# Attention and two feed-forward layers on one core: a fifth group in seven-product form, and weight blocks converted during the scores

## The chip, the cores and the metric

The kernel runs on one core of one Trainium2 chip. The metric is device time in microseconds of one execution; the kernel before has a median of 1001.72 us over three runs (1000.77 to 1002.63). The engines named below are TensorE (PE; PEld is its weight load), VectorE (DVE), ScalarE (ACT), GpSimd (POOL) and SyncE (SP, which issues nearly all transfers).

## The reference

Three stages over 6016 tokens of 256 channels, all in float32. The weights come in as float64, seen as pairs of 32-bit words.

```
qn = q / (norm(q over tokens) + 1e-6);  kn = likewise
s  = kn^T @ qn / tau                    # 256 x 256
a  = exp(s - max);  a = a / (a.sum + 1e-9)
x  = v @ a                              # 6016 x 256
x  = (relu(x @ w_in1) ** 2) @ w_out1    # d_ff 2048
y  = leaky(x @ w_in2, 0.01) @ w_out2
```

## The kernel before

**The scores.** q and k are loaded in 12 tiles (`qk`), eleven of 4 x 128 tokens (1 MB) and one of 3 x 128. TensorE accumulates k and q into the two halves of the scores (`sT`, L386), two records for one f32 product. ScalarE squares each tile (`sq`, L371), VectorE adds it to a running sum (`acc`, L376). At the last tile VectorE folds `acc` (L378) into `sums` (L379, L380), and TensorE sums it over the partitions (`pn`, four products with `ones`, eight records, L360); in TensorE's program these stand before the last two thirds of the last tile's score products. Then come the square root, reciprocals, the scaled scores, their transposes, the exponentials `e`, their transposes `eT`.

**Weights.** A float64 block is turned into float32 by a `Unit` (L124 on): ScalarE scales the high words (L143, `cm`), VectorE shifts, joins the sign, joins the low words (L146, L149, L153: the triple), ScalarE rounds to the high part (L192), VectorE takes the rest as the low part (`low`, L110). Each value is so held as two parts, and a product is three matmuls (high-high, high-low, low-high). `later` holds steps that are put behind the next tile's squares or additions. There are 16 blocks for the first layer: for each of 8 groups of 256 hidden channels an input block (`i`) and an output block (`o`).

**The fold.** x = v @ a is never formed: a is multiplied into w_in1, group by group (`pw`, L252, 12 matmuls of 256 columns), and scaled by the softmax's sums.

**The pairs.** The tokens go in six pairs of 448 or 512 tokens times two; each layer runs over the six pairs, each pair over the 8 groups. A group's first product, 256 channels by 256 hidden by two halves, is either plain, 8 block products of 3 matmuls (24, `h`, L704), or in seven-product form (Strassen's, 21 matmuls in the banks `ha` and `hb`, L543). The latter needs sums of weight blocks (VectorE L207 to L210 and a rounding of `wi`), sums of token blocks (`xr`), copies on ScalarE (L1504) and three additions on VectorE (L550). In the first pair the groups below `N0` are plain.

**What sets the order.** Up to the fold of group 0 the order is that of the code. Behind it a planner (`build`, `simulate`) places every instruction of the two layers on its engine by costs and due times, several rounds of it, and the best round is written out. `convert` gives a weight block's steps to it. SP issues transfers in program order, with eight lanes; a transfer waits for the one before it on its lane, and a tile of q and k for one of five buffers (`AHEAD`), free when TensorE and ScalarE are done with the tile. Three buffers (`wst`) hold raw weight blocks.

Of the kernel before, what the change touches and what calls it, by code (L numbers as in the profile page):

```python
# [28 lines left out]
def attn_moe_moe2(  # L29
# [12 lines left out]
    nc = tc.nc  # L42
# [192 lines left out]


    tiles = [(t0, min(G, T - t0)) for t0 in range(0, T, G)]
    PIECES = {0: ((0, 1), (1, 1), (2, 1), (3, 1)), **{n: ((0, 2), (2, 2)) for n in (1, 2, 3)}}
    NS = len(tiles)
    AHEAD = 5  # L240
    sT = [bank("ab"[j], f"sT{j}") for j in range(KC)]
# [52 lines left out]
    def converted(units):  # L294

        for u in units:
            later[ACT].append(u.scaled)
            yield
            for step in (u.shifted, u.sign, u.high):
                step()  # L300
                if step == u.high:
                    later[ACT].append(u.round)
                    later[ACT].append(lambda u=u: later[DVE].append(u.low))
                yield

    def run(steps, n):
        for _ in range(n):
            next(steps, None)
# [4 lines left out]
    with (  # L313
# [17 lines left out]
        def load_qk(n):  # L331
            t = qk[n] = att4.tile([P, 2, G, C], F32, tag="qk", name="qk")
            for i, m in pieces(n):

                t0 = (tiles[n][0] + i) * P
                for a, x in enumerate((q, k)):
                    src = x[0][t0 : t0 + m * P, :].rearrange("(p g) c -> p g c", g=m)
                    (nc.scalar if a and n == 0 else nc.sync).dma_start(t[:, a, i : i + m], src)  # L338

        for n in range(AHEAD):  # L340
            load_qk(n)
            if n == 3:
                first_i[0].load()
        tiny = small[:, 6, 0:1]
        nc.vector.memset(tiny, 1e-36)
        nc.scalar.activation(small[:, 7, 0:1], ones, AF.Square)
# [2 lines left out]

        for _ in range(6):  # L350
            nc.tensor.matmul(warm[:, :P], zeros, zeros, start=True, stop=True)
        steps = [converted([u]) for u in first_i]

        STEPS = {2: 1, 3: 3}

        def norm_sums():

# [7 lines left out]
        for n, (t0, g) in enumerate(tiles):  # L365
            t = qk.pop(n)
            last_tile = n == NS - 1

            sq = att2.tile([P, 2, G, C], F32, tag="sq", name="sq") if n else acc
            for i, m in pieces(n):  # L370
                nc.scalar.activation(part(sq, i, m), part(t, i, m), AF.Square)  # L371
            if last_tile:
                nc.scalar.activation(small[:, 7, 0:1], ones, AF.Sqrt)
            flush(ACT)
            if n:
                tt(part(acc, 0, g), part(acc, 0, g), part(sq, 0, g), op=ALU.add)  # L376
            if last_tile:
                tt(part(acc, 0, 2), part(acc, 0, 2), part(acc, 2, 2), op=ALU.add)  # L378
                tt(sums_[:, :C], acc[:, 0, 0], acc[:, 0, 1], op=ALU.add)  # L379
                tt(ordered(sums_[:, C:]), in_order(acc[:, 1, 0]), in_order(acc[:, 1, 1]), op=ALU.add)  # L380
            flush(DVE)
            for i in range(g):
                if last_tile and i == g - 2:
                    norm_sums()
                for j in range(KC):
                    nc.tensor.matmul(  # L386
                        sT[j][:, :C],
                        t[:, 0, i, j * P : (j + 1) * P],
                        t[:, 1, i],
                        start=n == 0 and i == 0,  # L390
                        stop=last_tile and i == g - 1,
                    )
            run(steps[0], STEPS.get(n, 0))
            if n + AHEAD < NS:
                load_qk(n + AHEAD)
            elif n + AHEAD == NS:
                first_i[1].load()
                load_first_v(0)
                load_first_v(1)
                nc.sync.dma_start(tau_sb, tau.partition_broadcast(P))  # L400
                first_o.load()
                others[0].load()

        xa, xb = x_tile(2, 1, 0), x_tile(1, 1, 0)

# [24 lines left out]

        nc.vector.reciprocal(rtau, tau_sb)

        run(steps[1], 1)
        flush(ACT)
        run(steps[1], 2)
        y, m, z, r = (small[:, i] for i in range(4))
        nc.scalar.activation(y, pn[:, :4], AF.Sqrt, bias=tiny, scale=0.25)
        nc.scalar.activation(small[:, 7, 0:1], ones, AF.Exp)
# [10 lines left out]
        sTs = [att.tile([P, C], F32, name=f"sTs{j}") for j in range(KC)]  # L449
        ts(ordered(sTs[0]), in_order(sT[0][:, :C]), r[:, 0:1], rtau, op0=ALU.mult, op1=ALU.mult)  # L450
        nc.scalar.activation(ordered(sTs[1]), in_order(sT[1][:, :C]), AF.Copy, scale=rq1)
        run(steps[1], 1)
        others[1].load()
        s = [bank("e", "s0"), bank("y3", "s1")]
        x_transpose(0, 0, "y1")
        x_transpose(1, 0, "y2", range(2))
# [421 lines left out]
    TAIL = 12  # L878
    TURNS = 14
    FIRST_MIXED = min([p for L, p in GROUPS if L == 1], default=0)  # L880
    CONV_BEGIN, CONV_END = 1.4, 4
    N0 = 4
    FOLD_AFTER = "F1"
    LOAD = 22
    VDUE = 30, 60
# [101 lines left out]
    def build(base):  # L987
# [12 lines left out]
        def T(*a, **k):  # L1000
            return Task(*a, **k)
# [55 lines left out]
            return t  # L1057

        whl_done = {0: None, 1: None}
        for i, u in enumerate([first_o, *others]):  # L1060
            n = u.g - 1 if u.kind == "i" else u.g + 1
            m, at0 = in_pair0(n)
            due = at0(m["fold"] if u.kind == "i" else m["second"][u.g > 0][0])
            t = convert(u, due - 35 - (0 if i else 10), loaded=wst_b.get(i))
            if u.kind == "i":
                whl_done[u.g] = t
            else:
                wo_ready[1, 0, u.g] = t
# [875 lines left out]
```

## Time and profile before

| | |
|---|---|
| median of three runs | 1001.72 us |
| the profiled execution: time, span | 1002.93 us, 1001.1 us |
| TensorE busy | 994.6 us, 99% of the span |
| VectorE busy | 901.4 us, 90% |
| ScalarE busy | 804.4 us, 80% |
| granted TensorE clock, mean | 1.000 |
| share of TensorE in the chain that ended last | 97% |

A matmul's row shows its latency (0.38 us for 512 columns), while a new one begins every 0.23 us, so records overlap and a merged row of n is shorter than n times the mean. Idle time stands in brackets ahead of a row, with what ended it.

### The profile page before, as it was taken

The numbers are of one execution on the slowest core, as the hardware profiler recorded it, in microseconds if no ns is written. First come the engines' busy times: TensorE is split into PE (matmuls) and PEld (weight loads), VectorE is DVE, ScalarE is ACT, GpSimd is POOL, SyncE is SP. The second block draws the span as 40 slices with busy tenths as digits, with TensorE's granted clock in tenths as the row PEclk, the third lists the DMA queues.
The fourth block names the chain that finished last, engine by engine and source line by source line (L and its number), as shares of the span: only waits on it lengthen the run. The fifth ranks groups of instructions, "written<-read, shape, count | busy, mean of one in ns | idle before, by whom it ended". The sixth has DMA issues, their size and how long they took to land.

```text
span 1001.1 us, 13148 instructions
## 1 busy us (share of the span) xinstructions
PE 994.6 (99%) x4528; PEld 837.3 (84%) x4528; DVE 901.4 (90%) x1314; ACT 804.4 (80%) x1184; POOL 0.7 (0%) x6
## 2 busy tenths in 40 slices
PE   9999999999999999999999999999999999999998
PEld 7888888887888888998888888888888888998887
DVE  4899999988988977999999999999999999998985
ACT  6799978877878777888898888779788788887773
POOL 0000000000000000000000000000000000000000
PEclk9999999999999999999999999999999999999999
DMA  9786559788978967965665665666577586676553
GB/s 339 281 253 205 200 193 287 266 308 296 332 284 294 318 249 265 316 219 206 223 209 200 229 215 202 201 217 226 172 219 233 182 239 227 210 233 220 195 143 84
DMA packets 160946, 234.97 MB, mean 235 GB/s; under 512 B 53232, under 2 KB 97264, under 8 KB 158576
## 3 DMA queue, kind: packets, MB, share of 16 engines
q1 hardware_dynamic: 160160, 233.48, 69.0%
q8 instruction: 36, 0.59, 0.2%
q10 hardware_dynamic: 720, 0.66, 0.2%
q14 instruction: 30, 0.25, 0.1%
HBM read 187.70 MB, written 46.40 MB: 234 GB/s over the span
## 4 chain that ended last, share of the span: by engine, by line
PE 97%; DMA 2%; DVE 0%; ACT 0%; ACTq 0%; issue 0%; SPq 0%
PE y L543 37%; PE ha L543 21%; PE hb L543 16%; PE yA L543 7%; PE yF L543 3%; PE hc L543 3%; PE sT L386 3%; PE he L543 2%; PE h L704 2%; PE pw L252 1%; DMA qk<-in_k_dram 1%; DMA qk<-in_q_dram 1%; PE y L587 0%; DVE o L552 0%; ACT e L472 0%; ACTq L338 0%
## 5 line engine op out<-in xcount | busy, mean ns | idle before, releaser
L543 PE MATMUL y<-g,wo 128*128 128x512 f32 (+1 forms) x1344 | 350.5, 387 | 0.0
L543 PEld LDWEIGHTS y<-g,wo 128*128 128x128 f32 x1344 | 252.1, 188 | 49.5 <-DVE wo L110 0.4
L543 PE MATMUL ha<-x,wi 128*128 128x512 f32 (+1 forms) x960 | 265.6, 385 | 0.0
L110 DVE TENSOR_TENSOR g<-c,g 128x1024 fp32r<-128x1024 f32 (+1 forms) x192 | 228.0, 1197 | 18.7 <-ACT g L674 13.9
L543 PEld LDWEIGHTS ha<-x,wi 128*128 128x128 f32 x960 | 180.0, 188 | 33.8 <-ACT c L1504 0.7
L543 PE MATMUL hb<-x,wi 128*128 128x512 f32 (+1 forms) x720 | 199.6, 386 | 0.1
L543 PEld LDWEIGHTS hb<-x,wi 128*128 128x128 f32 x720 | 134.3, 188 | 26.2 <-DVE c L550 1.7
L1612 DVE TENSOR_TENSOR c<-c 128x512 f32<-128x512 f32 (+1 forms) x208 | 139.9, 672 | 7.1 <-ACT c L691 1.2
L1587 ACT CAST g<-c 128x1024 fp32r<-128x1024 f32 (+1 forms) x104 | 105.2, 1023 | 5.1 <-PE y L543 2.4
L110 DVE TENSOR_TENSOR b<-c,b 128x512 fp32r<-128x512 f32 (+1 forms) x156 | 102.5, 668 | 2.0 <-ACT b L1605 1.7
L1605 ACT CAST b<-c 128x512 fp32r<-128x512 f32 (+1 forms) x156 | 93.1, 608 | 10.5 <-DVE c L1612 4.7
L681 ACT ACTIVATE c<-c 128x1024 f32<-128x1024 f32 (+1 forms) x96 | 100.0, 1043 | 1.5
L674 ACT CAST g<-c 128x1024 fp32r<-128x1024 f32 (+1 forms) x88 | 91.7, 1044 | 1.6
L1504 ACT COPY w<-ha 128x512 f32<-128x512 f32 (+1 forms) x80 | 46.2, 577 | 49.9 <-PE ha L543 49.6
L691 ACT ACTIVATE c<-c 128x512 f32<-128x512 f32 (+1 forms) x98 | 60.7, 621 | 8.8 <-DVE c L552 8.5
L1504 ACT COPY u<-ha 128x512 f32<-128x512 f32 (+1 forms) x80 | 46.0, 575 | 9.8 <-PE ha L543 6.9
L110 DVE TENSOR_TENSOR x<-xr,x 128x1024 fp32r<-128x1024 f32 (+3 forms) x47 | 49.1, 1051 | 0.6 <-ACT x L1261 0.6
L386 PE MATMUL sT<-qk 128*128 128x256 f32 x188 | 42.1, 382 | 1.4 <-DMA qk<-in_k_dram 1.3
L543 PE MATMUL yA<-g,wo 128*128 128x512 f32 (+1 forms) x156 | 42.9, 383 | 0.0
L543 PE MATMUL yF<-g,ws 128*128 128x512 f32 (+1 forms) x156 | 42.9, 383 | 0.0
L543 PE MATMUL y<-b,ws 128*128 128x512 f32 (+1 forms) x156 | 42.9, 383 | 0.0
L543 PE MATMUL y<-b,wo 128*128 128x512 f32 (+1 forms) x156 | 42.8, 383 | 0.0
(137 smaller groups left out, 1202.4 us busy)
## 6 DMA issues: line engine op xcount, KB each, us to landing
wi<-wi SPq DMA_DIRECT2D x88, 896.0 KB, 5.6
wo<-wo SPq DMA_DIRECT2D x84, 512.0 KB, 4.5
ws<-wo SPq DMA_DIRECT2D x120, 128.0 KB, 4.0
wst<-in_moe_w_in_dram SPq DMA_DIRECT2D x16, 512.0 KB, 6.0
wst<-in_moe_w_out_dram SPq DMA_DIRECT2D x16, 512.0 KB, 6.8
wi<-wis SPq DMA_DIRECT2D x8, 896.0 KB, 6.1
wo<-wis SPq DMA_DIRECT2D x7, 1024.0 KB, 7.6
wo<-wos SPq DMA_DIRECT2D x13, 512.0 KB, 5.8
```

The source lines that it names most:

```text
L110: tt(lo, x, raw(hi), op=ALU.subtract)
L252: nc.tensor.matmul(pw[:, i * 2 * P : (i + 1) * 2 * P], eT[:, a, j, i * P : (i + 1) * P], whl[g][:, b, j], start=t == 0 and (i == 0 or g == 0),
L386: nc.tensor.matmul(sT[j][:, :C], t[:, 0, i, j * P : (j + 1) * P], t[:, 1, i], start=n == 0 and i == 0, stop=last_tile and i == g - 1,)
L543: nc.tensor.matmul(ps, a[m], b[n], start=first and i == 0, stop=i == 2, skip_group_check=True)
L674: nc.scalar.copy(g_t[n, half][:, 0, :, :w], c)
L681: nc.scalar.activation(c, c, AF.Square)
L691: nc.scalar.activation(c, c, AF.Prelu, alpha=0.01)
L704: nc.tensor.matmul(h_t[n, half, fb][:, :w], a[i], b[j], start=start, stop=stop, skip_group_check=True)
L1504: nc.scalar.copy(to, h(0))
L1587: nc.scalar.copy(g_t[n, name][:, 0, :, :w], result(n, half, w))
L1605: nc.scalar.copy(b_t[n, name][:, 0, :w], c(half, fb))
L1612: tt(c(*to), c(*a), c(*b), op=ALU.subtract)
```

## The change

Four things are changed together.

- `N0` goes from 4 to 3: group 3 of the first pair is in seven-product form too, five groups of eight in place of four. Its folded weights are made in the form with sums, and the second pair has one group less that must still make them.
- The loads: tile 1's k goes out on ScalarE's queue as tile 0's does, and tile 3 is loaded and squared in one piece instead of two.
- Input block 0 was loaded ahead of tile 4 and converted at tiles 2 and 3; input block 1 and output block 0 were loaded behind the last tile. Now all three are loaded behind tiles 6, 8 and 10 and converted on the way: the scaling is put at n = 5, 7, 9, the triple at n = 6, 8, 10, the rounding one tile later. The two pieces of input block 1's conversion that stood in the softmax's chain are gone, and the planner no longer places output block 0's.
- Two numbers of the planner (`CONV_BEGIN`, `CONV_END`), the stretch in which the second layer's blocks are converted, and the due time of one block.

```
-    PIECES = {0: ((0, 1), (1, 1), (2, 1), (3, 1)), **{n: ((0, 2), (2, 2)) for n in (1, 2, 3)}}
+    PIECES = {0: ((0, 1), (1, 1), (2, 1), (3, 1)), **{n: ((0, 2), (2, 2)) for n in (1, 2)}}
...
-                    (nc.scalar if a and n == 0 else nc.sync).dma_start(t[:, a, i : i + m], src)
+                    (nc.scalar if a and n <= 1 else nc.sync).dma_start(t[:, a, i : i + m], src)
         for n in range(AHEAD):
             load_qk(n)
-            if n == 3:
-                first_i[0].load()
...
-        steps = [converted([u]) for u in first_i]
-
-        STEPS = {2: 1, 3: 3}
+        head_units = [*first_i, first_o]
+        steps = [converted([u]) for u in head_units]
+        LOADS = {1: 0, 3: 1, 5: 2}
+        STEPS = {5: (0, 1), 6: (0, 3), 7: (1, 1), 8: (1, 3), 9: (2, 1), 10: (2, 3)}
...
-            run(steps[0], STEPS.get(n, 0))
+            if n in STEPS:
+                i, m = STEPS[n]
+                run(steps[i], m)
             if n + AHEAD < NS:
                 load_qk(n + AHEAD)
+                if n in LOADS:
+                    head_units[LOADS[n]].load()
             elif n + AHEAD == NS:
-                first_i[1].load()
                 load_first_v(0)
                 load_first_v(1)
                 nc.sync.dma_start(tau_sb, tau.partition_broadcast(P))
-                first_o.load()
                 others[0].load()
+            elif n + AHEAD == NS + 2:
+                others[1].load()
...
-        run(steps[1], 1)
         flush(ACT)
-        run(steps[1], 2)
...
-        run(steps[1], 1)
-        others[1].load()
+        others[2].load()
...
-    CONV_BEGIN, CONV_END = 1.4, 4
-    N0 = 4
+    CONV_BEGIN, CONV_END = 1.2, 4.3
+    N0 = 3
...
-        for i, u in enumerate([first_o, *others]):
+        wo_ready[1, 0, 0], wo_b[1, 0, 0] = None, Buf("wo", 4, -8)
+        stores["o", 1, 0] = T("SP", "wo", -5, first_o.store, uses=[wo_b[1, 0, 0]], lat=LOAD)
+        for i, u in enumerate(others):
...
-            t = convert(u, due - 35 - (0 if i else 10), loaded=wst_b.get(i))
+            t = convert(u, due - 35, loaded=wst_b.get(i))
```

VectorE from the start of the scores to the last of the running sums, before; `acc` is the sum of squares, `cm` a weight block's words, `whl` its two parts, `sums` what `pn` reads:

```order
L376 TENSOR_TENSOR acc<-acc,sq 128x2048 x3
L146 TENSOR_SCALAR cm<-cm 128x512
L149 SCALAR_TENSOR_TENSOR cm<-wst,cm 128x512
L153 SCALAR_TENSOR_TENSOR cm<-wst,cm 128x512
L376 TENSOR_TENSOR acc<-acc,sq 128x2048
L110 TENSOR_TENSOR whl<-cm,whl 128x512
L376 TENSOR_TENSOR acc<-acc,sq 128x2048 x6
L376 TENSOR_TENSOR acc<-acc,sq 128x2x768
L378 TENSOR_TENSOR acc<-acc 128x2x512
L379 TENSOR_TENSOR sums<-acc 128x256
L380 TENSOR_TENSOR sums<-acc 128x256
L431 RECIPROCAL rtau<-tau_sb 128x1
```

The same engine now, from the second block's triple on (lines behind L340 have moved by one or two); ahead of it stand six additions in a row, the first block's triple, one addition, its `low` and one addition:

```order
L146 TENSOR_SCALAR cm<-cm 128x512
L149 SCALAR_TENSOR_TENSOR cm<-wst,cm 128x512
L153 SCALAR_TENSOR_TENSOR cm<-wst,cm 128x512
L375 TENSOR_TENSOR acc<-acc,sq 128x2048
L110 TENSOR_TENSOR whl<-cm,whl 128x512
L375 TENSOR_TENSOR acc<-acc,sq 128x2048
L146 TENSOR_SCALAR cm<-cm 128x512
L149 SCALAR_TENSOR_TENSOR cm<-wst,cm 128x512
L153 SCALAR_TENSOR_TENSOR cm<-wst,cm 128x512
L375 TENSOR_TENSOR acc<-acc,sq 128x2x768
L377 TENSOR_TENSOR acc<-acc 128x2x512
L378 TENSOR_TENSOR sums<-acc 128x256
```

Before, one block lay between the third and the fifth addition; now three lie behind the sixth, the last of them directly ahead of the last tile's addition and the sums.

SP's queue around the weight blocks, before (tile 3 in two pieces, a block, tile 4, tile 5):

```order
L338 DMA qk_171<-in_q_dram 128x512
L338 DMA qk_171<-in_k_dram 128x512
L138 DMA wst_176<-in_moe_w_in_dram 128x2x512
L338 DMA qk_178<-in_q_dram 128x1024
L338 DMA qk_178<-in_k_dram 128x1024
L338 DMA qk_203<-in_q_dram 128x1024
```

and now (from the end of tile 6 to the last tile's q):

```order
L338 DMA qk_214<-in_k_dram 128x1024
L138 DMA wst_217<-in_moe_w_in_dram 128x2x512
L338 DMA qk_231<-in_q_dram 128x1024
L338 DMA qk_231<-in_k_dram 128x1024
L338 DMA qk_245<-in_q_dram 128x1024
L338 DMA qk_245<-in_k_dram 128x1024
L138 DMA wst_248<-in_moe_w_in_dram 128x2x512
L338 DMA qk_261<-in_q_dram 128x1024
L338 DMA qk_261<-in_k_dram 128x1024
L338 DMA qk_275<-in_q_dram 128x1024
L138 DMA wst_278<-in_moe_w_out_dram 128x2x512
L338 DMA qk_296<-in_q_dram 128x768
```

The first block moved from ahead of tile 4 to behind tile 6, and two more from behind the last tile to ahead of tiles 9 and 11.

TensorE at group 3 of the first pair, before (from the fold of that group's neighbour on; `h` is a plain first product):

```order
L252 MATMUL pw<-whl,eT 128x256 x12
L704 MATMUL h<-x_373,wi 128x512 x3
L704 MATMUL h<-x_374,wi 128x512 x3
L543 MATMUL y<-g,wo 128x512 x6
L704 MATMUL h<-x_373,wi 128x512 x3
L704 MATMUL h<-x_374,wi 128x512 x3
L543 MATMUL y<-g,wo 128x512 x9
```

and now (`ha` and `hb` are the banks of the seven-product form; the two rows from `x_779` and `x_801` are one block product):

```order
L543 MATMUL ha<-x_388,wi 128x512 x3
L252 MATMUL pw<-whl,eT 128x256 x12
L543 MATMUL hb<-x_389,wi 128x512 x3
L543 MATMUL y<-g,wo 128x512 x3
L543 MATMUL ha<-x_774,wi 128x512 x3
L543 MATMUL y<-g,wo 128x512 x3
L543 MATMUL hb<-x_728,wi 128x512 x3
L543 MATMUL ha<-x_779,wi 128x512 x2
L543 MATMUL ha<-x_801,wi 128x512
L543 MATMUL y<-g,wo 128x512 x3
```

In the whole program TensorE has 24 matmuls fewer in `h` and 21 more in `ha` and `hb`.

## Rows read from the trace of the kernel before

**Rows 1.** The head of the page: span and instructions.
```profile
span 1001.1 us, 13148 instructions
```
**Rows 2.** Busy by stretch: us, then each engine's busy us (records), clock, DMA.
```profile
53.00:150.00 97.00, 96.98 (x465) 81.24 (x465) 93.00 (x150) 84.71 (x126) 0.00 (x0) 1.00 0.64 214
150.00:1002.00 852.00, 847.57 (x3822) 712.93 (x3820) 772.28 (x1121) 683.57 (x1017) 0.00 (x0) 1.00 0.69 233
```
**Rows 3.** Timeline, TensorE: start us, length us, line, operation, [idle before it].
```profile
1.08 2.93 PE L351 MATMUL warm<-zeros 128*128 128x128 f32 x12 [1.08 <-DVE small L345]
...
20.05 25.28 PE L386 MATMUL sT<-qk 128*128 128x256 f32 x116 [0.30 <-DMA qk<-in_k_dram]
45.16 0.95 PE L360 MATMUL pn<-ones,sums 128*128 128x1 f32 x8
...
48.87 1.26 PE L422 MATMUL x<-ident,v_in_order 128*128 128x128 f32 x10
...
52.95 3.01 PE L704 MATMUL h<-x,wi 128*128 128x512 f32 x12
55.98 1.70 PE L252 MATMUL pw<-whl,eT 128*128 128x256 f32 x12
57.52 8.35 PE L704 MATMUL h<-x,wi 128*128 128x512 f32 x36
65.70 2.88 PE L543 MATMUL y<-g,wo 128*128 128x512 f32 x12
```
**Rows 4.** Timeline, ScalarE: squares of tiles 3, 4 and 6, the square root.
```profile
16.18 1.06 ACT L371 ACTIVATE sq<-qk 128x1024 f32<-128x1024 f32 x1 [0.26 <-DMA qk<-in_k_dram]
...
20.01 1.91 ACT L371 ACTIVATE sq<-qk 128x2048 f32<-128x2048 f32 x1 [1.96 <-DMA qk<-in_k_dram]
...
25.14 1.91 ACT L371 ACTIVATE sq<-qk 128x2048 f32<-128x2048 f32 x1 [0.68 <-DMA qk<-in_k_dram]
...
46.14 0.26 ACT L437 ACTIVATE small<-pn,small 128x4 f32<-128x4 f32 x1 [2.13 <-PE pn L360]
```
**Rows 5.** Timeline, VectorE: a block's rounding, tiles 5 and 6, the sums.
```profile
24.17 0.69 DVE L110 TENSOR_TENSOR whl<-cm,whl 128x512 fp32r<-128x512 f32 x1
24.77 4.69 DVE L376 TENSOR_TENSOR acc<-acc,sq 128x2048 f32<-128x2048 f32 x2
...
42.56 1.23 DVE L378 TENSOR_TENSOR acc<-acc 128x1024 f32<-128x1024 f32 x1
43.82 0.43 DVE L379 TENSOR_TENSOR sums<-acc 128x256 f32<-128x256 f32 x1
44.16 0.42 DVE L380 TENSOR_TENSOR sums<-acc 128x256 f32<-128x256 f32 x1
```
**Rows 6.** Groups by shape, VectorE, 0 to 53 us: busy us, mean ns, idle before.
```profile
L376 DVE TENSOR_TENSOR acc<-acc,sq 128x2048 f32<-128x2048 f32 x10 | 22.9, 2293 | 14.4 <-ACT sq L371 14.3
L376 DVE TENSOR_TENSOR acc<-acc,sq 128x1536 f32<-128x1536 f32 x1 | 1.8, 1758 | 0.1
L149 DVE SCALAR_TENSOR_TENSOR cm<-wst,cm 128x512 uint32<-128x512 uint32 x2 | 1.4, 698 | 0.1
...
L146 DVE TENSOR_SCALAR cm<-cm 128x512 uint32<-128x512 uint32 x2 | 0.8, 413 | 0.0
```
**Rows 7.** Groups by shape, VectorE, 53 to 150 us.
```profile
L110 DVE TENSOR_TENSOR wi<-wr,wi 128x1024 fp32r<-128x1024 f32 x4 | 4.8, 1210 | 0.0
...
L550 DVE CUSTOM_DVE_ANT_0 c<-u,hb 128x512 f32<-128x512 f32 x5 | 3.4, 685 | 0.6 <-PE hb L543 0.5
...
L210 DVE TENSOR_TENSOR wr<-wr 128x128 f32<-128x128 f32 x6 | 1.7, 291 | 0.2
```
**Rows 8.** Waits of weight loads: us in total, times, longest.
```profile
PEld hb L543 <- DVE c L550: 1.7, 5, 0.5
...
PEld pw L252 <- DVE x L110: 0.4, 1, 0.4
```
**Rows 9.** Busy by stretch, the end of the span.
```profile
1000.00:1002.00 2.00, 0.00 (x0) 0.00 (x0) 0.00 (x0) 0.00 (x0) 0.00 (x0) 0.68 0.00 0
```

## The prediction

> **What bounds the kernel now.** I read the page's head first: the profiled execution has a span of 1001.1 us [rows 1] and was timed at 1002.93 us, so 1.8 us lie around the span. The median of the three timed runs is 1001.72 us, 1.21 us below the profiled one; I make the sum against 1002.93 and take 1.21 off at the end.
>
> Next the busy time by stretch [rows 2]: from 53 us to 150 us TensorE is busy 96.98 of 97 us, and from 150 us on it is idle for little more than the output's tail. VectorE is busy 93.00 of those 97 us as well. So what counts is, first, how much work TensorE has, and, second, whether VectorE or a transfer makes it wait.
>
> Then TensorE's own timeline [rows 3]. From 20.05 us the score products run without a break, 116 of them in 25.28 us, 0.216 us each (one 128x256 product of f32 is two records). At 45.16 us come the eight records of the norm sums (`pn`), and at 52.95 us the first products of the first pair. A 512-wide product costs 0.227 us: 36 of them begin at 57.52 us and the next row at 65.70 us.
>
> The norm sums need VectorE's running sum of squares `acc`. Its last step before them, L380, ends at 44.16+0.42 = 44.58 us [rows 5], just before TensorE wants it. That hand-over is the place to watch: before it VectorE follows the loads, and behind it everything is a chain (`pn`, a square root on ScalarE at 46.14 us which had waited 2.13 us for `pn` [rows 4], reciprocals, the scaled scores, the softmax, the fold) that TensorE cannot shorten.
>
> **The change part by part.**
>
> *Group 3 of the first pair in seven-product form.* Its first product goes from 24 products of 512 columns to 21. Three times 0.227 us [rows 3] is 0.7 us less on TensorE, all of it on the path, since TensorE is idle 0.02 us in that stretch [rows 2]. VectorE gets three additions of 0.68 us, four small sums of 0.29 us and a rounding of 1.21 us in place of two folded roundings: at most 2.04+1.16+1.21 = 4.4 us [rows 7]. It loses there what now lies ahead of the scores' end: all four steps of the first output block, 0.41+0.70+0.70+0.69 = 2.5 us (its third step is of the second's form), and the last step of the second input block, 0.69 us [rows 5, 6]. The balance is +1.2 us at most in 97 us, of which VectorE has 4 us free [rows 2]. I cost it at nothing; if that cover is gone, TensorE waits for the difference, 1.2 us. Group 3's prepared operands are wanted one group earlier, and they also stand earlier in VectorE's order.
>
> *The first loads.* The loads fill the queue during the scores: ScalarE starts the squares of tile 4 at 20.01 us and those of tile 6 at 25.14 us, 2.57 us for each tile of 1 MB, every one behind a wait for its transfer [rows 4]. The weight block ahead of tile 4 shows as the larger step from 16.18 us (the second half of tile 3) to 20.01 us: 3.83 - 2.57 = 1.26 us for 512 KB. With that block moved behind tile 6, tiles 4 to 6 land 1.26 us earlier, and TensorE's wait of 0.30 us ahead of tile 4 [rows 3] goes. Tile 1's second operand goes out on ScalarE's queue, which delays ScalarE's first squares by some 2 us; ScalarE still waits for its loads at tile 3 [rows 4], so that is caught up. Behind tile 6 come three blocks, 3.8 us of transfer, where there were none, but each tile is needed 3.45 us (16 x 0.216) after the last and lands 2.57 us after it, so TensorE does not wait for them. By itself this is worth 0.3 us up to the 1.3 us that the block cost, and it is lost again at the next step.
>
> *Three blocks converted during the scores.* Per block VectorE does 0.41 + 0.70 + 0.70 us and, a tile later, a rounding of 0.69 us [rows 5, 6]. Before, one block was done in that time, ahead of the addition of tile 5, with VectorE then idle until tile 6's squares: tile 6's addition starts at 24.77+4.69-2.29 = 27.17 us [rows 5]. Now all three stand behind that addition, and the triple of the third stands right ahead of the addition of the last tile. I add VectorE's work up from there. Tile 6's addition starts 1.26 us earlier, at 25.9 us. Then:
> - five additions of 2.29 us: 11.5 us [rows 6]
> - the last tile's, of 1.76 us [rows 6]
> - three triples of 1.81 us: 5.4 us
> - two of the three roundings, 1.4 us (the third stands behind the sums)
> - the closing sums, 1.23 + 0.43 + 0.34 us: 2.0 us [rows 5]
>
> That is 22.1 us. Neighbours that do not depend on each other overlap by 0.09 us in these rows (24.77 us against 24.17+0.69), some seven times here, so 21.5 us; the end is at 47.4 us, 2.8 us later than 44.58. None of the inputs is later than that: the slowest, the third block, has its turn on ScalarE near 40 us, and VectorE reaches it near 41.5 us.
>
> TensorE came to `pn` at 45.16 us and now comes some tenths earlier, so it waits. What is queued behind `pn` on TensorE is the last eight score records, the transposes and the fold; behind them everything. Of the 2.8 us, 0.4 us are slack that the sums had (45.16 - 44.58, less some 0.2 us for the weight load of `pn`), and 0.3 us come back because half of the four `pn` products need only the first of the two last sums. I take +2.1 us. Bounds: -0.3 us, if VectorE is not late after all, and +2.8 us, if neither the slack nor the split counts.
>
> *Behind the sums.* The fold of group 1 at 55.98 us begins 0.3 us after the 12 products ahead of it are through (52.95 + 12 x 0.227 = 55.67), and the weight load's wait is put down to VectorE [rows 3, 8]. One rounding (0.69 us) that stood ahead of the operand it waits for is gone, so these 0.3 us go: -0.3 us. After that the planner writes another order for the whole program. What it now makes TensorE wait for is small (the largest entry, weight loads waiting for VectorE's L550, is 1.7 us in five places over the span [rows 8]); I bound this by 1.7 us to either side and take nothing.
>
> Sum: +2.1 - 0.3 - 0.7 = +1.1 us, or 1004.0 us against the profiled 1002.93 and **1002.8 us** against the median.
>
> The clock is where a wait of this size could cost more than itself. The granted clock is 1.00 through the work [rows 2] and falls to half only behind the end: 0.68 as the mean of the last stretch, after TensorE had stopped [rows 9]. At the start the 12 records of 128 columns take 2.93 us, and later 10 of the same size 1.26 us [rows 3]: the lower and the upper level, 1.2 and 2.4 GHz. The Trainium skill, in "TensorE: Matmul & The Clock Gate", section "Part 1: The HAM clock gate (the 'warmup' mystery)", says the same as a rule: the full clock is held by activity, and idling gives it up. By that rule a wait in mid-program, of which this trace has none of such a size, can lower the clock; it speaks against this change, and the second rival takes it up.
>
> **The rivals.**
>
> *VectorE is in time (1000.4 us).* For it: VectorE sat idle for 14.3 us in front of these additions [rows 6], more than the 6.8 us that are added behind tile 6. Against it: the blocks stand behind tile 6, where an addition comes with the loads every 2.57 us and takes 2.29 us, so that five of them leave 1.4 us for 6.8 us of added work. Then the wait at `pn` is not there, and 0.3 (tile 4) + 0.3 + 0.7 us are won: 1001.72 - 1.3.
>
> *The clock falls in the wait (1005.6 us; slower).* Place: the wait ahead of `pn`, some 2.4 us long. Price: the products from there to the first pair run at half speed. The last eight score records cost 8 x 0.216 = 1.7 us more, and the transposes, the softmax's and the fold's products about 1.1 us more where they are on the chain: +2.8 us on top of +1.1. It decides from the point where the wait is long enough for the clock to fall; for it is the fall behind the end, against it that the clock stayed at 1.00 over the wait of 0.30 us ahead of tile 4 [rows 2, 3]; how long a wait must be, no row shows.
>
> *The first pair no longer fits VectorE (1004.5 us; slower).* For it: 93 of 97 us are taken already [rows 2], and five groups in a row now bring the additions. Against it: the sum above is nearly level. Price: the 1.7 us that the new order may cost, on top of +1.1.
>
> *The change saves nothing in products.* That group 3 is still computed in 24 products is excluded by the order, which has three records fewer.
>
> **How the numbers follow.** Two runs of this kernel are told apart from about 0.2%, 2.0 us, on. Chances: the forecast 0.62, VectorE in time 0.16, the clock 0.10, the first pair 0.12. The forecast alone lies within 1001.3 to 1004.2 (its wait between 1.3 and 2.8 us, the new order some tenths). For 8 in 10 I reach to half of the first rival and to most of the others: 1000.2 to 1005.5 us. Faster by over 2.0 us (below 999.7) needs the first rival and a better order besides: 0.06. Slower by over 2.0 us (above 1003.7) is most of the clock's and the first pair's share and a seventh of the forecast's: 0.29. Between them 0.65.
>
> **What would show it.** Right: `pn` begins near 47 us with an idle TensorE of over 2 us ahead of it, put down to VectorE's last sums; VectorE has no idle time from tile 6's addition to those sums; the first products of the pair begin near 55 us; TensorE stays gapless behind. Wrong: the sums end before 45.5 us (the ledger of VectorE is wrong); `pn` waits for a transfer (the blocks delay the tiles); the granted clock is below 1.00 between 44 and 60 us; TensorE is idle by over half a microsecond between 60 and 150 us.

## The result: slower by 0.64%, and the profile after

The changed kernel takes 1008.39 us in the median of six runs (1005.60 to 1009.73) against 1001.65 us (1000.77 to 1002.63) for the kernel before: a ratio of 1.0064, 95% interval 1.0049 to 1.0080. Forecast were 1002.8 us, with a range up to 1005.5.

The execution that was profiled is the fastest of the six, at 1005.60 us, and the one profiled of the kernel before, at 1002.93 us, is 1.3 us above that kernel's median. So these two traces lie 2.7 us apart, the medians 6.7 us: the traces show part of the loss. The span of the changed kernel's trace, and its busy time by stretch with the columns of [rows 2]:

```profile
span 1003.7 us, 13111 instructions
```

```profile
53.00:150.00 97.00, 96.82 (x466) 80.17 (x465) 92.54 (x152) 84.60 (x127) 0.00 (x0) 1.00 0.65 214
150.00:1002.00 852.00, 849.37 (x3831) 714.70 (x3829) 773.21 (x1121) 682.58 (x1016) 0.00 (x0) 1.00 0.69 232
```

TensorE is still the bound, and the clock is 1.00 in both stretches. Against [rows 2] TensorE's busy time has lost 0.16 us in the first pair; the finer count under "The experiments", which sees gaps too short to show as idle time, has 1.0 us.

TensorE's timeline, the rows that answer to [rows 3]:

```profile
9.07 35.66 PE L385 MATMUL sT<-qk 128*128 128x256 f32 x164 [0.72 <-DMA qk<-in_k_dram]
46.46 1.05 PE L359 MATMUL pn<-ones,sums 128*128 128x1 f32 x8 [1.73 <-DVE sums L378]
47.38 1.97 PE L385 MATMUL sT<-qk 128*128 128x256 f32 x8
...
52.16 0.98 PE L478 MATMUL eT<-ident,e 128*128 128x128 f32 x4 [0.63 <-ACT e L472]
53.12 1.69 PE L252 MATMUL pw<-whl,eT 128*128 128x256 f32 x12
54.66 3.06 PE L704 MATMUL h<-x,wi 128*128 128x512 f32 x12
57.55 1.59 PE L252 MATMUL pw<-whl,eT 128*128 128x256 f32 x12
```

The score products run from 9.07 us without a break, so no weight block delays a tile that TensorE wants. Then TensorE idles for 1.73 us until VectorE's sums are there. `pn` starts at 46.46 us instead of 45.16, the pair's first products at 54.66 instead of 52.95: 1.71 us later. The larger part, 1.30 us, is the wait. The other 0.41 us lie between `pn` and those products.

VectorE's timeline from tile 6's addition to the sums; the last rows answer to [rows 5]:

```profile
24.76 2.29 DVE L375 TENSOR_TENSOR acc<-acc,sq 128x2048 f32<-128x2048 f32 x1 [0.25 <-ACT sq L370]
...
29.34 2.29 DVE L375 TENSOR_TENSOR acc<-acc,sq 128x2048 f32<-128x2048 f32 x1 [0.49 <-ACT sq L370]
...
38.94 2.29 DVE L375 TENSOR_TENSOR acc<-acc,sq 128x2048 f32<-128x2048 f32 x1
41.14 0.42 DVE L146 TENSOR_SCALAR cm<-cm 128x512 uint32<-128x512 uint32 x1
41.60 0.69 DVE L149 SCALAR_TENSOR_TENSOR cm<-wst,cm 128x512 uint32<-128x512 uint32 x1
42.33 0.69 DVE L153 SCALAR_TENSOR_TENSOR cm<-wst,cm 128x512 uint32<-128x512 uint32 x1
42.94 1.75 DVE L375 TENSOR_TENSOR acc<-acc,sq 128x1536 f32<-128x1536 f32 x1
...
46.33 0.42 DVE L379 TENSOR_TENSOR sums<-acc 128x256 f32<-128x256 f32 x1
```

Behind 29.34 us VectorE has no idle row up to the sums' end at 46.33 + 0.42 = 46.75 us, 2.17 us later than 44.58. The third block's triple, the three steps of VectorE from 41.14 to 43.02 us, stands directly in that path.

The second place is 365 us. TensorE's and ScalarE's timelines there:

```profile
365.33 0.84 PE L543 MATMUL y<-g,wo 128*128 128x512 f32 x3
366.87 0.97 PE L543 MATMUL ha<-x,wi 128*128 128x512 f32 x3 [0.70 <-ACT c L1506]
```

```profile
363.25 1.05 ACT L1404 CAST wis<-wr 128x1024 fp32r<-128x1024 f32 x1 [1.19 <-DMA wi<-wis]
364.20 1.05 ACT L681 ACTIVATE c<-c 128x1024 f32<-128x1024 f32 x1
365.29 1.05 ACT L674 CAST g<-c 128x1024 fp32r<-128x1024 f32 x1
366.24 0.58 ACT L1506 COPY c<-ha 128x512 f32<-128x512 f32 x1
```

ScalarE's rounding `wis` waits 1.19 us for a buffer that a transfer is still storing, three steps are queued behind it, and TensorE waits 0.70 us for the last of them, a copy. The planner's order put them there. By itself this wait doesn't tell the two traces apart: behind 150 us the changed kernel's loses 2.4 us in all, that of the kernel before 2.1.

### The profile page after: what moved, and what is told of

It reads as the page before. It is cut to its first block, busy times and chain, and to the rows that moved or that the text cites. A ratio compares the mean times of both kernels' runs of the same rounds, so it can differ in the third digit from the quotient of the medians.

```text
span 1003.7 us, 13111 instructions
## 1 busy us (share of the span) xinstructions
PE 994.9 (99%) x4525; PEld 837.1 (83%) x4525; DVE 903.0 (90%) x1314; ACT 802.9 (80%) x1183; POOL 0.7 (0%) x6
## 4 chain that ended last, share of the span: by engine, by line
PE 93%; DMA 3%; DVE 2%; ACT 1%; issue 1%; SPq 0%; ACTq 0%
PE y L543 36%; PE ha L543 21%; PE hb L543 16%; PE yA L543 7%; PE yF L543 3%; PE hc L543 3%; PE he L543 2%; DMA qk<-in_k_dram 2%; PE h L704 2%; PE pw L252 1%; DMA wi<-wis 1%; DVE acc L375 1%; PE sT L385 1%; PE y L587 0%; ACT sq L370 0%
## 5 line engine op out<-in xcount | busy, mean ns | idle before, releaser
L543 PE MATMUL ha<-x,wi 128*128 128x512 f32 (+1 forms) x972 | 269.4, 385 | 0.7 <-ACT c L1506 0.7
L543 PE MATMUL hb<-x,wi 128*128 128x512 f32 (+1 forms) x729 | 202.3, 386 | 0.2
```

The costliest lines, as they stand in the source:

```text
L543: nc.tensor.matmul(ps, a[m], b[n], start=first and i == 0, stop=i == 2, skip_group_check=True)
```

## The experiments

Fifteen runs, each of five or more executions, always beside the kernel before on the same chip (medians 1001.1 to 1001.6 us, from chip to chip; a distance from the kernel before is taken below from the run's own). The table holds the runs' medians, the ratio with its interval, and from each one's trace four numbers: the end of the sums, the start of the pair's first products, and what TensorE lost between those and 150 us, and behind 150 us. "Lost" is, summed over its records, the distance from one start to the next less the usual distance for that shape; so it also counts gaps too short to show as idle time, and products slowed by a fallen clock. Four of the traces have the same order on TensorE behind the head (before, x8, x11, x12): they lose 0.7 to 0.8 us up to 150 us and 0.9 to 2.1 behind it. A difference of about 1 us in the last column therefore says little.

| kernel | us | ratio | sums end | first products | lost to 150 | lost behind |
|---|---|---|---|---|---|---|
| before | 1001.65 | 1 | 44.58 | 52.95 | 0.8 | 2.1 |
| changed | 1008.39 | 1.0064 (1.0049 to 1.0080) | 46.75 | 54.66 | 1.8 | 2.4 |
| x1_again | 1007.97 | 1.0065 (1.0053 to 1.0077) | 47.94 | 57.55 | 1.8 | 2.0 |
| x2_fill | 1006.71 | 1.0044 (1.0031 to 1.0057) | 47.13 | 55.04 | 1.8 | 3.5 |
| x3_head | 1009.50 | 1.0075 (1.0062 to 1.0087) | 47.12 | 56.73 | 0.7 | 5.1 |
| x4_planner | 1007.09 | 1.0055 (1.0043 to 1.0067) | 44.12 | 52.79 | 3.8 | 3.0 |
| x5_third_late | 1006.47 | 1.0050 (1.0038 to 1.0063) | 45.58 | 54.79 | 2.1 | 3.6 |
| x6_n0_alone | 1006.30 | 1.0046 (1.0033 to 1.0060) | 43.49 | 52.56 | 3.7 | 3.6 |
| x7_conv_alone | 1001.67 | 1.0006 (0.9997 to 1.0014) | 43.43 | 52.17 | 0.4 | 2.3 |
| x8_loads_alone | 1001.73 | 1.0007 (0.9999 to 1.0016) | 43.29 | 52.24 | 0.8 | 1.0 |
| x9_third_in_softmax | 1003.72 | 1.0026 (1.0016 to 1.0036) | 44.92 | 52.51 | 2.0 | 2.4 |
| x10_three_groups | 1004.50 | 1.0032 (1.0019 to 1.0044) | 44.10 | 52.62 | 0.7 | 3.0 |
| x11_sums_late | 1003.26 | 1.0023 (1.0013 to 1.0033) | 47.20 | 56.48 | 0.7 | 0.9 |
| x12_late_and_fill | 1003.57 | 1.0026 (1.0015 to 1.0036) | 46.37 | 54.29 | 0.7 | 0.9 |
| x13_softmax_four | 1003.98 | 1.0028 (1.0018 to 1.0038) | 45.78 | 53.39 | 0.5 | 5.1 |
| x14_softmax_four_conv | 1004.48 | 1.0028 (1.0018 to 1.0037) | 44.98 | 52.70 | 0.8 | 2.3 |
| x15_softmax_five_old | 1011.74 | 1.0098 (1.0084 to 1.0111) | 45.29 | 52.90 | 2.2 | 10.4 |

**x1_again: the changed kernel, unchanged.**

> The changed kernel once more, to see whether its runs differ by the granted clock. Theory C (in most runs the clock falls to half in or behind the wait ahead of the norm sums): runs from 1005 to 1010 us, the mean granted clock of a run goes with its time, the slow ones at 0.996 to 0.998, and a trace of a slow one shows a stretch below 1.00 between 44 and 60 us and longer products there. Theory L (later transfers vary, such as the store that a cast waits for near 363 us): the clock is 1.00 in the slow runs up to the end, and the waits differ behind 300 us.

Measured: 1007.97 us. This trace holds what the first one lacked. TensorE's timeline, and its busy time in three stretches (columns of [rows 2]):

```profile
47.66 1.18 PE L359 MATMUL pn<-ones,sums 128*128 128x1 f32 x8 [2.96 <-DVE sums L378]
48.70 3.53 PE L385 MATMUL sT<-qk 128*128 128x256 f32 x8
```

```profile
44.00:48.00 4.00, 1.04 (x7) 0.62 (x6) 3.93 (x6) 2.70 (x5) 0.00 (x0) 1.00 0.49 143
48.50:51.80 3.30, 3.30 (x9) 2.70 (x10) 1.23 (x9) 1.75 (x3) 0.00 (x0) 0.50 0.03 7
52.00:56.00 4.00, 3.25 (x26) 2.51 (x24) 2.41 (x8) 2.69 (x7) 0.00 (x0) 1.00 0.01 2
```

The same eight score records that took 1.97 us in the fastest run take 3.53 us: behind a wait of 2.96 us the granted clock is 0.50, the lower of the two levels, and back at 1.00 from 52 us. From the sums' end to the first products it is 57.55 - 47.94 = 9.61 us, against 54.66 - 46.75 = 7.91 us in the fastest run: a price of 1.7 us. The mean granted clock of the eleven executions of the changed kernel is 0.996 to 0.998 in ten and 0.999 in the fastest, and 1.000 (0.999 at least) in those of the kernel before. A mean doesn't tell where the clock fell: x1's trace alone shows the place, and x2 tests it for the others.

**x2_fill: TensorE kept busy in the wait.**

```
                 if last_tile and i == g - 2:
+                    for _ in range(8):
+                        nc.tensor.matmul(warm[:, :P], zeros, zeros, start=True, stop=True)
                     norm_sums()
```

> Eight products of zeros (128 columns, sixteen records, 1.75 us) are put ahead of the norm sums, where TensorE otherwise sits idle for 1.7 us; nothing else changes. Theory C: the slow runs vanish, all lie within 1004.5 to 1006.5 us, the clock at 0.999 or above. Theory L: no change, median near 1008, the same spread. If the wait itself is all the loss, 1005.6 as the fastest run of before.

Measured: 1006.71 us, mean clock 0.999 or 1.000 in all five executions. The timeline:

```profile
44.28 1.95 PE L384 MATMUL warm<-zeros 128*128 128x128 f32 x16
46.85 1.05 PE L359 MATMUL pn<-ones,sums 128*128 128x1 f32 x8 [0.62 <-DVE sums L378]
47.76 1.97 PE L387 MATMUL sT<-qk 128*128 128x256 f32 x8
```

The sums are as late as before (47.13 us), but the idle time is 0.62 us, the eight records take 1.97 us again, and 7.91 us later the first products start. With TensorE kept busy in the wait, none of the five executions has a mean clock below 0.999. The fall so belongs to the idle wait, and is worth 1.3 us between the medians and 1.7 us on the chain.

**x3_head and x4_planner: either half of the change alone.** The changed kernel with the planner's old numbers, and the old head with `N0` = 3 and the new numbers.

```
-    CONV_BEGIN, CONV_END = 1.2, 4.3
-    N0 = 3
+    CONV_BEGIN, CONV_END = 1.4, 4
+    N0 = 4
```

> The change's loads and its three blocks during the scores, with the planner's numbers of before (four groups in seven-product form, the second layer's blocks in the old stretch). Theory C: spread and slow runs as in the changed kernel, median 1007 to 1009. Theory L (the planner's new order makes the loss): 1003 to 1004, VectorE's delay of 1.7 us alone, with a spread under 2 us.

> The other half: the loads and conversions of before, and the planner's new numbers (five groups in seven-product form, the second layer's blocks in the new stretch). Theory C: 1001 to 1002.5, a spread under 2 us, the 0.7 us of three products gained and some of it lost to waits. Theory L: 1005 to 1008.

Measured: 1009.50 and 1007.09 us, 7.9 and 5.5 us above the kernel before: one half alone costs more than both together (6.3 us in x1), the other nearly as much. In x3 the clock falls behind an idle time of 1.68 us, and TensorE loses 5.1 us behind 150 us. In x4 the head is whole (first products at 52.79 us) and TensorE loses 3.8 us up to 150 us. So the halves don't add up, and the planner's order is not the small term that I took it for.

**x5_third_late: the third block's triple behind the sums.**

```
-        STEPS = {5: (0, 1), 6: (0, 3), 7: (1, 1), 8: (1, 3), 9: (2, 1), 10: (2, 3)}
+        STEPS = {5: (0, 1), 6: (0, 3), 7: (1, 1), 8: (1, 3), 9: (2, 1), 11: (2, 3)}
```

> The changed kernel with one edit: the triple of the third weight block (three steps, 1.8 us on VectorE) stands behind the sums instead of ahead of the last tile's addition; the order of TensorE and SP is the same in every row. Theory A (the head costs two terms, a late hand-over and a fallen clock): the sums end about 1.8 us earlier, near 45.2 us, the wait ahead of pn is below 0.5 us, no record shows the clock below 1.0, the first products of the pair begin near 53 us; 1.7 + 1.7 us less than the changed kernel, so 1004.5 us, and what is left above the kernel before is the planner's. Rival B (the clock falls because of the small products that stand there in any case, not because of the wait): the clock still falls near 46 us and the time is 1006.3. Rival C (the loads set the sums' end, VectorE's work only fills up the gaps): sums at 46.5 or later, 1007.5.

Measured: 1006.47 us. Sums 1.2 us earlier than in the changed kernel's first trace, a wait of 0.90 us, no fall of the clock, and the first products still at 54.79 us. ScalarE's timeline tells why:

```profile
47.40 0.62 ACT L192 CAST wo<-cm 128x512 fp32r<-128x512 f32 x1 [2.15 <-DVE cm L153]
47.93 0.26 ACT L438 ACTIVATE small<-pn,small 128x4 f32<-128x4 f32 x1
```

The block's rounding, which waits for VectorE's triple, now stands ahead of the square root, which could have begun 1.5 us sooner (in x9 it begins 1.09 us behind `pn`'s start, here 2.63). The lateness had moved to another engine. None of the three theories had that.

**x6_n0_alone and x7_conv_alone: the planner's two edits apart**, each on the kernel before.

```
x6:  -    N0 = 4                          +    N0 = 3
x7:  -    CONV_BEGIN, CONV_END = 1.4, 4   +    CONV_BEGIN, CONV_END = 1.2, 4.3
```

> The kernel before with N0 = 3 alone: head, loads and the stretch for the second layer's blocks as before. Theory A (any new number gives the planner an order that was not picked out, and such an order makes TensorE wait 2 to 5 us more): head as before, sums at 44.3 us, clock 1.0, TensorE's waits behind 53 us 2 to 5 us more, less 0.7 us for three products: 1003 to 1006. Rival B (the loss is in the two numbers of the stretch for the conversions): waits as before, 1001.0. Rival C (VectorE has no room for a fifth group in the first pair): waits of over 1 us between 53 and 150 us, put down to VectorE.

> The kernel before with CONV_BEGIN 1.2 and CONV_END 4.3 alone; four groups in seven-product form in the first pair, as before. Theory A (any new number costs): waits behind 53 us 2 to 5 us more than before, 1003 to 1006, nearly all behind 150 us. Rival B (the stretch is the cause of the loss): 1006 to 1007, as with both planner changes. Rival C (only N0 costs): 1001.7.

Measured: 1006.30 us and 1001.67 us. The stretch costs nothing, though it gives a new order too; the fifth group costs 0.46%. VectorE and TensorE of x6 near 145 us:

```profile
143.50 1.22 DVE L110 TENSOR_TENSOR x<-xr,x 128x1024 fp32r<-128x1024 f32 x1
144.64 1.22 DVE L110 TENSOR_TENSOR g<-c,g 128x1024 fp32r<-128x1024 f32 x1
145.77 0.68 DVE L110 TENSOR_TENSOR wo<-cm,wo 128x512 fp32r<-128x512 f32 x1
```

```profile
144.50 0.86 PE L543 MATMUL ha<-x,wi 128*128 128x512 f32 x3
146.51 0.73 PE L543 MATMUL y<-g,wo 128*128 128x512 f32 x2 [1.15 <-DVE wo L110]
```

VectorE has no idle row from 134 us on, and TensorE waits 1.15 us for a weight block's rounding `wo` in its queue: with the old head, five groups and the planned conversions leave VectorE late in the first pair, though its busy time there is 93.55 us of 97 against 93.00 before. In the changed kernel 1.8 us are lost instead of 3.7, with three blocks converted during the scores; there it is small waits of weight loads, of up to 0.5 us, for VectorE's additions `c` and for ScalarE's copies.

**x8_loads_alone**: the first two hunks of the change on the kernel before.

> The kernel before with the two edits of the loads alone: tile 1's k on ScalarE's queue, tile 3 in one piece; the order of every row on TensorE and VectorE is that of before. Theory A (they only let tiles 1 to 3 land sooner; the block ahead of tile 4 still costs its 1.26 us): TensorE's first products run some tenths sooner, pn comes at most 0.4 us earlier, 1001.3 to 1001.7. Rival B (ScalarE issues a transfer in front of its squares and falls behind): the sums end later by up to 1 us, 1002.5.

Measured: 1001.73 us, no difference. The scores run from 3.80 us without a break, `pn` begins at 44.35 us:

```profile
3.80 40.71 PE L386 MATMUL sT<-qk 128*128 128x256 f32 x180
44.35 0.95 PE L360 MATMUL pn<-ones,sums 128*128 128x1 f32 x8
```

TensorE and VectorE do the same in the same order as in the kernel before, and this trace (1001.25 us) is near that kernel's median, so it is the better yardstick for the traces that follow.

**x9_third_in_softmax: the third block where the kernel before had its second.**

```
-        STEPS = {5: (0, 1), 6: (0, 3), 7: (1, 1), 8: (1, 3), 9: (2, 1), 10: (2, 3)}
+        STEPS = {5: (0, 1), 6: (0, 3), 7: (1, 1), 8: (1, 3)}
...
+        run(steps[2], 1)
         flush(ACT)
+        run(steps[2], 2)
...
+        run(steps[2], 1)
         others[2].load()
```

> The changed kernel with the third block's conversion where the kernel before had its second: scaling, shift and sign while VectorE waits for the square root, the third step behind the scaled scores, the rounding behind that. The order of TensorE and SP is the changed kernel's in every row. Theory A (in x5_third_late the sums came early, but the block's rounding on ScalarE stood ahead of the square root and kept 1.7 us; without that the head is nearly whole): the sums end near 45.4 us, the square root begins within 1.9 us of that, no record of a fallen clock, the first products of the pair near 53.4 us, 1005.1 us; what is left above the kernel before is the fifth group. Rival B (the softmax's chain has no room for the block either): first products at 54.8 us, 1006.5 us as in x5_third_late.

Measured: 1003.72 us, better than theory A had it, with the changed kernel's order on TensorE in every row. The timeline:

```profile
44.64 1.05 PE L359 MATMUL pn<-ones,sums 128*128 128x1 f32 x8
45.55 1.97 PE L385 MATMUL sT<-qk 128*128 128x256 f32 x8
...
52.51 3.02 PE L707 MATMUL h<-x,wi 128*128 128x512 f32 x12
```

No wait at `pn`, no fall of the clock, the first products as early as before. Above the kernel before on its own chip, x1 takes 1007.97 - 1001.64 = 6.3 us and x9 1003.72 - 1001.22 = 2.5 us, so that this one block's place is worth 3.8 us. The 2.5 us that are left lie behind the head: against x8's trace the one of x9 (1003.54 us) has its first products 0.3 us later, loses 1.2 us more up to 150 us and 1.4 us more behind it, and has 0.7 us less to do, together 2.2 us.

**x10_three_groups**: the kernel before with `N0 = 5`.

> The kernel before with N0 = 5, so three groups of the first pair in seven-product form, not four; three products more on TensorE. Theory A (the number of groups counts by VectorE's work in the first pair: five are too many, three leave it free): TensorE's waits between 60 and 150 us stay below 0.4 us, 0.7 us for the products, 1001.8 us. Rival B (any other number of groups than the one of before gives an order that makes TensorE wait, as N0 = 3 did with 2.9 us there and more later): waits of over 1.5 us, 1004 to 1006.

Measured: 1004.50 us. Up to 150 us TensorE loses 0.7 us, as theory A said; but behind it the trace loses 2.0 us more than that of x8 (the largest single losses are 0.65 us at 309 us and 0.45 us at 780 us), and the products cost 0.7 us. Each theory had half of it.

**x11_sums_late and x12_late_and_fill**: the kernel before with nothing but a delay ahead of the sums; then the same with the products of zeros of x2.

```
+            if last_tile:
+                for _ in range(4):
+                    tt(delay, delay, delay, op=ALU.add)
             if n:
                 tt(part(acc, 0, g), part(acc, 0, g), part(sq, 0, g), op=ALU.add)
```

> The kernel before, every row of it in the old order, with four additions of 128x512 zeros on VectorE ahead of the last tile's addition: nothing but a delay of the sums by about 2.6 us. Theory A (a late hand-over costs its length less the slack, and the clock falls behind the wait): the sums end at 46 to 47.2 us, TensorE idles 1.6 to 2.6 us ahead of pn, a record shows the clock at half for some microseconds behind it, the first products come at 56 to 57 us and the waits behind 60 us stay as before: 1001.2 + 2.0 + 1.7 = 1004.9 us. Rival B (the fall belongs to something else in the changed head): clock 1.0 throughout, 1003.2 us.

> As x11_sums_late, with eight products of zeros (128 columns) on TensorE directly ahead of pn, which run in the wait. Theory A: the wait is cut to under 1 us of idle time, no record of a fallen clock, sums as late as in x11_sums_late, first products near 55 us, 1003.2 us, 1.7 us less than x11_sums_late. Rival B (the clock plays no part): the same time as x11_sums_late.

Measured: 1003.26 and 1003.57 us. In two of x11's eight executions the mean clock is 0.998, and these take 1005.17 and 1005.28 us; in the other six it is 0.999 or 1.000 and they take 1002.48 to 1003.43. The profiled one is of the first kind:

```profile
46.92 1.05 PE L362 MATMUL pn<-ones,sums 128*128 128x1 f32 x8 [2.07 <-DVE sums L384]
47.84 3.66 PE L391 MATMUL sT<-qk 128*128 128x256 f32 x8
```

So in an order that is otherwise untouched, sums late by some 2.6 us (47.20 against 44.58) cost 1.7 us in the median of the six executions without a lowered clock (1002.91 against 1001.22), and some 2.3 us more in the two with one. It fell less often than I expected, so that the fill, behind which no execution is below 0.999, had nothing to win in the median.

**x13, x14, x15: who owns the 2.5 us that are left.** x9's head with `N0` = 4 and the old stretch, with `N0` = 4 and the new stretch, and with `N0` = 3 and the old stretch.

> As x9_third_in_softmax (two blocks converted during the scores, the third in the softmax's chain) with the planner's numbers of before: N0 = 4, CONV 1.4 and 4. Four groups in seven-product form, three products more than the changed kernel. Theory A (behind the head, the fifth group is what costs: 1.2 us of waits up to 150 us and some behind, against 0.7 us for its products): first products at 52.5 us, waits up to 150 us below 0.8 us, and behind 150 us 1 to 2.5 us: 1001.2 us, level with the kernel before. Rival B (taking output block 0 out of the planner spoils the order whatever N0 is, as the 5 us of waits behind 150 us in x3_head would have it): waits behind 150 us of 4 to 5 us, 1004 us.

> As x13_softmax_four, with CONV 1.2 and 4.3 as the changed kernel has it. Theory A (the fifth group costs, the stretch for the conversions does not, as x7_conv_alone had it): 1001.2 us, waits up to 150 us below 0.8 us. Rival B (output block 0 out of the planner spoils the order): 1004 us. A better result than 1000.5 us would be a version that beats both kernels: one block less for VectorE in the first pair, and nothing lost in the head.

> As x9_third_in_softmax, N0 = 3, with CONV 1.4 and 4 as before. Theory A (five groups cost by VectorE in the first pair): waits between the first products and 150 us of 1.5 to 2.5 us, as in x9_third_in_softmax, 1003 to 1004 us. Rival B (the waits there come from the particular order that CONV 1.2 and 4.3 gave): below 0.8 us, 1000.8 us.

Measured: 1003.98, 1004.48 and 1011.74 us. Theory A is right on the first pair: 0.5 and 0.8 us lost with four groups, 2.2 with five. It is wrong on the time: four groups are no faster, and x15 takes over 7 us more than either theory had. Each of these orders has one long wait behind 150 us. ScalarE and TensorE of x13, and TensorE of x15:

```profile
178.28 0.68 ACT L143 ACTIVATE cm<-wst 128x512 f32<-128x512 f32 x1 [2.79 <-DMA wst<-in_moe_w_out_dram]
...
182.49 0.57 ACT L1509 COPY c<-ha 128x512 f32<-128x512 f32 x1
```

```profile
183.11 1.43 PE L546 MATMUL ha<-x,wi 128*128 128x512 f32 x3 [1.86 <-ACT c L1509]
```

```profile
197.23 1.65 PE L546 MATMUL hc<-x,wi 128*128 128x512 f32 x3 [4.52 <-ACT c L1509]
```

A weight step on ScalarE waits for its transfer, the copy that TensorE needs stands some steps behind it, and behind TensorE's wait the clock is at 0.50 again (in x15 over 196 to 202 us). x13's trace is the slowest of its nine executions, and only two of them have a lowered mean clock; in x15 all five have. x14 has such a wait at 365 us (1.30 us), as the changed kernel has, behind a rounding that waits for its buffer.

Rival B's number came in: with output block 0 out of the planner, all four orders tried with the mended head are 2.5 us or more slower. That the block's leaving is the cause is not shown. x6, where the planner still places it, has the same kind of wait on ScalarE and TensorE:

```profile
362.17 1.05 ACT L192 CAST wis<-wr 128x1024 fp32r<-128x1024 f32 x1 [2.71 <-DMA wos<-wis]
```

```profile
367.37 0.96 PE L543 MATMUL ha<-x,wi 128*128 128x512 f32 x3 [1.06 <-ACT c L1504]
```

Of the new orders only x7's costs nothing. Which rule of the planner lets a waiting step stand ahead of such a copy was not tried. No version beat the kernel before.

## Why the prediction was wrong

- *The sums late on VectorE (+2.1 us).* Right in place and nearly in size. The ledger said 47.4 us; the traces of this head have 46.75 to 47.94. In the first of them two errors cancel in part: tile 6's addition came 1.1 us before the 25.9 us that the ledger starts from, and VectorE then waited 0.49 us for a tile's squares. In the profiled run the first products came 1.71 us later, and x11 puts 1.7 us on a like delay without the clock. "`pn` begins near 47 us", "no idle time on VectorE from tile 6's addition", "first products near 55 us": 46.46 us, one gap of 0.49 us, 54.66 us.
- *The clock (second rival, chance 0.10, price +2.8).* This is the step that failed first: the sum has the clock at nothing. I put it down as a side case because the clock had stayed at 1.00 over a wait of 0.30 us, though my own forecast was a wait seven times as long. By the mean clock it fell in ten of eleven executions; the price is 1.3 to 1.7 us, less than I gave, since in x1 nearly all of it falls on the eight score records (3.53 us instead of 1.97), and the transposes and the fold run at the full clock again. Of the Trainium skill, "TensorE: Matmul & The Clock Gate", section "Part 1: The HAM clock gate (the 'warmup' mystery)", the rule that activity gives the full clock and idling takes it away is borne out by the 0.50 of x1 behind 2.96 us of idle time and its absence in x2.
- *The planner's new order ("bound 1.7 us to either side, take nothing").* The second step that failed, and the larger: with the clock's 1.7 us the forecast of 1002.8 us would still have been inside its range, with this term it would not. With the head mended (x9) the change costs 2.5 us although three products are saved (0.7 us): 3.2 us of waits, of which the traces of x9 and x8 show 2.6. I had bounded an order by the largest wait of another order, and an order that hadn't run has no such bound: the new ones here lost 2.7 to 12.6 us in all, the old one 1.6 to 2.9. The third rival, "the first pair no longer fits VectorE", was right in part: 1.0 us more is lost up to 150 us, 2.9 us with the old head (x6). Behind 150 us, where this rival saw nothing, x9 loses another 1.4 us against x8. The level balance for VectorE came true (92.54 us busy against 93.00); it counted the work and not when it is due.
- *Three products fewer (-0.7 us).* Right: the distance from the first to the last product less what was lost is 941.82 us before and 941.14 after.
- *The fold's 0.3 us.* Hardly counted: the fold at 57.55 us still starts 0.17 us after the 12 products ahead of it are through (54.66 + 12 x 0.227 = 57.38), where it was 0.31 us.
- *The loads: early, and lost again at `pn`.* Right: the tiles land early (tile 6's addition at 24.76 us, where 25.9 was reckoned), TensorE waits at `pn` all the same, and x8 shows no gain from its two edits.

So the sum was +2.1 - 0.3 - 0.7 = +1.1 us. The medians of x1, x2 and x9 divide the 6.3 us of x1 into +2.6 for the late block without the clock, +1.3 for the clock and +2.5 for the order with its products. Of the first part x11 gives 1.7 us to a like delay of the sums, and 0.3 us can be named besides: in the changed head the exponentials `e` start 0.41 us behind the step `nb` of VectorE, in x9 0.10 us. The other 0.6 us are open.

## What to carry to other kernels

A saving at the bound (three products) is bought with work on an engine that is in front of a hand-over: ask for that hand-over's slack first, here 0.4 us against 6.8 us of added work. Where TensorE is made to wait in mid-program, count the clock as part of the price and look at several executions, since the one that is profiled may have escaped it. And where a change makes a planner write a new order, the old order's waits say nothing about the new one's: split the change so that one part leaves the order alone, as the head and the order could be split here.

## What the runs showed of the hardware

The clock's fall doesn't go by the length of the idle time alone: it fell behind 1.68 us (x3), 1.86 us (x13), 2.07 us (x11) and 2.96 us (x1), and not behind 1.73 us in the changed kernel's first trace. Of one kernel's executions (x11) the two with a lowered mean clock took some 2 us longer than the others.

In all five traces where no weight block's rounding stands ahead of the exponentials `e` on ScalarE (the changed kernel, x1, x2, x3, x5), `e` starts 0.41 to 0.42 us after the first `nb` ends on VectorE; in the others 0.1 us, and 0.22 us in x14. The semaphores waited for are the same; why it is later was not found.
